# A channel DFT in even and odd halves, mirrored rows on GpSimd, padded tiles and a new order of the steps

## The chip, the cores and the metric

One core of one Trainium2 chip runs the whole program. The metric is the device time of one execution, in microseconds (us). Executions differ by more than a fraction of a per cent, so kernels are compared as ratios of fast executions from the same rounds on the same chip, with a 95% interval. Faster and slower mean by over 2%.

## The reference

Eight batches, each of 576 rows, with 8 heads of 64 dimensions: an attention with exponential features, then on its output `x` (576 x 512) a Fourier mixing, a normalisation and a feed-forward with 2048 hidden units.

```python
proj = einsum('bhsd,df->bhsf', x, w_phi); proj -= max(abs(proj), axis=-1)      # q and k
phi  = concatenate([exp(proj), exp(-proj)], axis=-1)
x    = (q_phi @ (k_phi^T v)) / (q_phi . sum(k_phi) + 1e-6)
u    = x + real(fft(fft(x, axis=seq), axis=channel))
un   = (u - mean(u)) / sqrt(var(u) + 1e-6)
out  = u + relu(un @ w_ch1) @ w_ch2
```

## The kernel before

In this program TensorE multiplies matrices and leaves the products in PSUM tiles; VectorE, ScalarE and GpSimd do the work element by element, and what isn't in PSUM lies in the working memory SBUF. A DFT is a discrete Fourier transform. The program is software-pipelined by hand. Each stream of work has a letter: F the feed-forward, M attention and mixing, D the folding of rows, N the normalisation, P, T, R and S the attention features, K, V and Q loads that GpSimd issues, A and B transposing DMAs, C constants, G and J the first transposes. Three strings of letters (a start, a first period, a period that is repeated) give the order in which the steps of different batches are issued. A step whose inputs or tile slots aren't ready by the plan is held and tried again at the next letter. Each engine then works through its own queue in that order, and what stands first in the queue holds up the rest (halfmm_k_ahead below shows it: GpSimd's queue stood 37.2 us in all at eight loads).

```python
def weave(plan):
    held = []
    for name in plan:
        held = [x for x in held if not step(x)]
        if name in held or not step(name):
            held.append(name)
...
BUFS = {"pj": 2, "pk": 1, "pb": 3}          # PSUM tiles; psf, pso and pu all come from pb
```

The part that is changed most is the channel DFT with the residual add. `DT` and `ET` hold the sequence transform, `CD` and `SD` are the cosine and sine matrices, `X` is the residual in SBUF (fp32), `C` = 512. Because of the symmetry of a real input one PSUM tile `pu` serves a direct row tile and its mirrored one, whose channels are read backwards.

```python
for t in range(3):
    M = 128 if t < 2 else 64
    pu = pb.tile([128, C], F32)
    ... 4 matmuls of 512 columns: DT.CD + ET.SD                       # L737
    if t < 2:
        nc.vector.tensor_tensor(out=X[:, t, 0:C], in0=pu[:], in1=X[:, t, 0:C], op=ALU.add)          # L742
        nc.vector.tensor_tensor(out=X[:, 2 + t, 1:C], in0=pu[:, C - 1:0:-1], in1=X[:, 2 + t, 1:C], op=ALU.add)   # L745
        nc.vector.tensor_tensor(out=X[:, 2 + t, 0:1], in0=pu[:, 0:1], in1=X[:, 2 + t, 0:1], op=ALU.add)
    else:
        nc.vector.tensor_tensor(out=X[0:64, 4, 0:C], in0=pu[0:64, :], in1=X[0:64, 4, 0:C], op=ALU.add)
```

After it come the statistics and the centred rows `UN` on VectorE, a transposing DMA to `UT`, the square roots `VE` and `rs` on GpSimd, and then the two matmul layers: `psf` (288 columns) from `UT`, and `pso` (512 columns), which VectorE adds to `X` (L832).

The softmax here doesn't subtract the row's maximum and nothing guards it: scores larger than these inputs give would overflow.

## Time and profile before

| | before |
|---|---|
| time | 461.1 us (456.46 to 462.73, 3 runs) |
| span of the profiled run, granted TensorE clock | 457.1 us, 0.946 |
| TensorE busy, idle (span less busy) | 409.4, 47.7 us |
| one steady period | 49.46 us, of which TensorE is busy 48.30, VectorE 38.83, ScalarE 36.11, GpSimd 33.63 |

The prediction below shows how these rows are read.

### The profile page before, as it was taken

To read this page: it belongs to the slowest core of one execution; us is meant where nothing else is said; L and a number is where in the kernel's file an instruction comes from. 1 tells how busy PE (TensorE), PEld (TensorE's weight loads), DVE (VectorE), ACT (ScalarE), POOL (GpSimd) and SP (SyncE) were. 2 spreads that over 40 slices of the span, in tenths; PEclk is the share of its full clock that TensorE was granted. 3 is DMA by queue.
4 is the path that set the end of the run, shared out by engine and by line. 5 is a ranking of instruction groups with operands and counts; after the bars stand their busy time and mean duration, and the time that the engine had idled before them with its cause. 6 is when DMAs were issued, how large, how long until landed. Compare 5 with 4: busy or idle time off the path is not lost.

```text
span 457.1 us, 10115 instructions
## 1 busy us (share of the span) xinstructions
PE 409.4 (90%) x3941; PEld 249.9 (55%) x3964; DVE 322.3 (71%) x597; ACT 303.2 (66%) x651; POOL 267.4 (58%) x357
## 2 busy tenths in 40 slices
PE   4586358889998999999999999999999999999994
PEld 3364125664367545764477436854576448645741
DVE  6868675695987678885887678877888585658012
ACT  5877468767865976587766885697658776621810
POOL 4867779369259683787367764778379433901000
PEclk9855576999999999999999999999999999999999
DMA  7699959905469086956599099908793052006004
GB/s 208 154 201 136 191 92 102 165 13 52 77 138 142 12 87 121 157 55 53 99 153 113 3 120 128 170 1 86 122 155 58 4 104 51 1 15 119 22 12 92
DMA packets 111087, 43.26 MB, mean 95 GB/s; under 512 B 85313, under 2 KB 105921, under 8 KB 111041
## 3 DMA queue, kind: packets, MB, share of 16 engines
q0 software_dynamic: 45936, 16.60, 34.4%
q1 hardware_dynamic: 65105, 26.03, 32.4%
q8 instruction: 31, 0.51, 0.5%
q14 instruction: 15, 0.12, 0.1%
HBM read 36.77 MB, written 9.44 MB: 101 GB/s over the span
## 4 chain that ended last, share of the span: by engine, by line
PE 65%; DMA 11%; DVE 9%; ACT 6%; POOL 5%; issue 2%; SPq 0%; DVEq 0%; ACTq 0%; POOLq 0%
PE pso L826 24%; PE psf L814 16%; PE pu L737 4%; DMA UT<-UN 3%; DMA QT<-QS 3%; PE psD L715 3%; PE kv L637 3%; PE pso L841 2%; PE psh L547 2%; POOL FEO L599 2%; DMA KT<-KS 2%; ACT HT L819 2%; PE psk L441 2%; PE psq L497 2%; ACT KPp L447 1%
## 5 line engine op out<-in xcount | busy, mean ns | idle before, releaser
L814 PE MATMUL psf<-UT,W1b 128*128 128x288 bf16 x1024 | 148.9, 288 | 6.9 <-DMA UT<-UN 4.6
L819 ACT ACTIVATE HT<-psf 128x288 bf16<-128x288 f32 x256 | 103.3, 413 | 57.9 <-PE psf L814 48.9
L826 PE MATMUL pso<-W2b,HT 128*128 128x512 bf16 x491 | 118.8, 380 | 1.4 <-issue 0.8
L814 PEld LDWEIGHTS <-W1b 128*128 128x128 bf16 x1024 | 92.5, 98 | 32.3 <-issue 10.0
L826 PEld LDWEIGHTS <-HT 128*128 128x128 bf16 x512 | 46.5, 98 | 56.5 <-issue 6.9
L667 POOL TENSOR_TENSOR X<-cb,rd 128x320 f32<-128x320 f32 x64 | 46.4, 729 | 35.8 <-DVE rd L666 35.8
L832 DVE SCALAR_TENSOR_TENSOR X<-pso,rs,X 128x512 f32<-128x512 f32 x32 | 24.0, 749 | 53.7 <-PE pso L826 53.6
L599 POOL TENSOR_TENSOR FEO<-X 128x320 f32<-128x320 f32 x59 | 49.6, 862 | 2.2
L416 POOL TENSOR_TENSOR VCn<-VS,VCn 128x512 bf16<-128x512 bf16 x28 | 29.8, 1066 | 34.3 <-ACT VCn L412 32.6
L505 DVE TENSOR_REDUCE MQ<-psq 128x8 f32<-128x1024 f32 (+1 forms) x40 | 39.4, 1005 | 10.3 <-PE psq L497 10.1
L461 DVE TENSOR_REDUCE MK<-psk 128x8 f32<-128x1024 f32 x32 | 38.5, 1218 | 6.7 <-ACT KPp L447 4.8
L788 POOL TENSOR_SCALAR VE<-MV 128x5 f32<-128x5 f32 x8 | 3.9, 488 | 65.4 <-DVE MV L766 65.3
L556 ACT ACTIVATE QPHP<-psh 128x1024 bf16<-128x1024 f32 x32 | 33.0, 1030 | 7.6 <-PE psh L547 7.5
L447 ACT ACTIVATE KPp<-psk 128x1024 bf16<-128x1024 f32 x32 | 32.6, 1019 | 1.4 <-PE psk L441 1.1
L447 ACT ACTIVATE KPn<-psk 128x1024 bf16<-128x1024 f32 x32 | 32.6, 1018 | 1.0 <-DVE MK L461 1.0
L556 ACT ACTIVATE QPHN<-psh 128x1024 bf16<-128x1024 f32 x32 | 33.1, 1036 | 0.0
L416 POOL TENSOR_TENSOR VCp<-VS,VCp 128x512 bf16<-128x512 bf16 x28 | 31.2, 1114 | 0.0
L645 ACT CAST kvh<-kv 128x130 bf16<-128x130 f32 x64 | 17.4, 272 | 20.3 <-PE kv L641 20.3
L652 PEld LDWEIGHTS <-QPHP 128*128 128x128 bf16 x320 | 24.8, 102 | 5.5 <-DVE cb L664 4.3
L765 DVE BATCH_NORM_STATS2 st<-X 128x6 f32<-128x512 f32 (+1 forms) x40 | 27.4, 685 | 0.3
L652 PEld LDWEIGHTS <-QPHN 128*128 128x128 bf16 x320 | 23.2, 99 | 1.3 <-issue 0.2
L237 POOL DMA_DIRECT2D QS<-in_q_dram x28 | 23.1, 837 | 0.3 <-issue 0.3
(404 smaller groups left out, 746.9 us busy)
## 6 DMA issues: line engine op xcount, KB each, us to landing
out_dram<-X SPq DMA_DIRECT2D x64, 64.0 KB
out_dram<-X SPq DMA_DIRECT2D x16, 256.0 KB
KS<-in_k_dram POOLq DMA_DIRECT2D x14, 256.0 KB, 7.3
QS<-in_q_dram POOLq DMA_DIRECT2D x14, 256.0 KB, 5.0
VS<-in_v_dram POOLq DMA_DIRECT2D x7, 512.0 KB, 9.7
W1b<-in_moe_w_ch_dram POOLq DMA_DIRECT2D x1, 2048.0 KB, 12.9
W2b<-in_moe_w_ch_dram POOLq DMA_DIRECT2D x1, 2048.0 KB, 21.4
W2b<-in_k_dram SPq DMA_DIRECT2D x2, 512.0 KB
```

The lines of the kernel that those rows point to most:

```text
L416: nc.gpsimd.tensor_tensor(out=VC[:, hs, :, 0:D], in0=values[b][0][:, hs, :].rearrange("p h (j d) -> p h j d", d=D), in1=VC[:, hs, :, D:D + ...
L447: nc.scalar.activation(out=KP[:, hs, :, :].rearrange("p e (jp jj) f -> p jj (e jp) f", jj=2), in_=psk[:], func=AT.Exp, scale=sgn,)
L461: nc.vector.tensor_reduce(out=MK[:, 2 * pr:2 * pr + 2, :].rearrange("p e (jp jj) -> p jj (e jp)", jj=2), in_=tiles[pr][:], axis=AX.X, op=A ...
L505: nc.vector.tensor_reduce(out=o, in_=i[:], axis=AX.X, op=ALU.max, apply_absolute_value=True)
L556: nc.scalar.activation(out=o, in_=psh[:], func=AT.Exp, scale=sgn)
L599: eng.tensor_tensor(out=FEO[:, :, i, a:a + D], in0=X[:, :, a:a + D], in1=X[:, :, C - a:C - a - D:-1], op=op,)
L652: nc.tensor.matmul(pn_[:, i, 65 * c:65 * c + 65], lhsT=QP[:, h, 128 * c:128 * c + 128], rhs=kvh[:, i, :], start=True, stop=True,)
L667: nc.gpsimd.tensor_tensor(out=X[:, :, D * h:D * h + D], in0=cb[:, :, 0:D], in1=rd[:].to_broadcast([128, 5, D]), op=ALU.mult,)
L765: nc.vector.bn_stats(out=st[0:M, :], in_=X[0:M, c, 0:C])
L814: nc.tensor.matmul(ps[:], lhsT=W1b[:, cc, 128 * hh:128 * hh + 128], rhs=UT[:, cc, 288 * hf:288 * hf + 288], start=(cc == 0), stop=(cc == N ...
L819: nc.scalar.activation(out=HT[:, hh, 288 * hf:288 * hf + 288], in_=ps[:], func=AT.Relu)
L826: nc.tensor.matmul(po[:], lhsT=HT[:, hh, 128 * c:128 * c + 128], rhs=W2b[:, hh, :], start=(hh == 0), stop=(hh == NHH - 1),)
```

## The change

Its intent: fewer columns on TensorE in the channel DFT. The cosine part is even in the channel and the sine part odd, so 257 and 255 columns suffice, and sum and difference of the two give both halves of a row. The diff, cut to its core:

```diff
-START = "CGGTCRTGGRJJGSSTTTWC ... "      # all plans are new; the last three batches get their own
+START = "PGGTDSTCSTCCGTGQRJGT ... "
+LAST = "KRMFFTMFMFMFMPFMPFMF ... "
-        weave(START + FIRST + PERIOD * (B - 1))
+        weave(START + FIRST + PERIOD * (B - 3) + LAST)
...
+            if b:
+                half_channels(X, FEO, t)
+                yield
+                continue
...
+    def half_channels(X, FEO, t):
+        pu = pb.tile([128, C], F32, tag="pb", name="pu")
+        n = C // 2
+        ... 3 matmuls of 257 columns into pu[:, 0:n+1], 2 of 255 into pu[:, n+1:C]
+        nc.scalar.copy(out=QO[0:M], in_=pu[0:M, n + 1:C])                              # L798, to SBUF
+        for i, op in enumerate((ALU.add, ALU.subtract)):
+            nc.vector.tensor_tensor(out=PQ[0:M, i, 1:n], in0=pu[0:M, 1:n], in1=QO[0:M], op=op)   # L801
+        nc.scalar.copy(out=PQ[0:M, 0, 0:n + 1:n], in_=pu[0:M, 0:n + 1:n])              # L804
+        adds = [(nc.vector, X[0:M, c, 0:n + 1], PQ[0:M, 0, :]),
+                (nc.vector, X[0:M, c, n + 1:C], PQ[0:M, 1, n - 1:0:-1])]
+        if t < 2:
+            adds += [(nc.gpsimd, X[:, 2 + t, 1:n], PQ[:, 1, 1:n]),
+                     (nc.gpsimd, X[:, 2 + t, n:C], PQ[:, 0, n:0:-1]),
+                     (nc.gpsimd, X[:, 2 + t, 0:1], PQ[:, 0, 0:1])]
+        for eng, x, y in adds:
+            eng.tensor_tensor(out=x, in0=x, in1=y, op=ALU.add)                         # L817
```

`QO` and `PQ` lie in SBUF, in the room of `FEO`. Besides: the one-row and one-column matmuls `pm` and `px` and the 64-row `pu` become full tiles, the big K load is issued ahead of the small one at the start, four 960-element constants move from VectorE to GpSimd, and eight small exponentials a batch become four. Batch 0 keeps the full channel DFT.

## The prediction

> **What bounds the kernel now.** I read the page's busy shares first, then the slices, the chain that ended last, the stretches of one steady period, and last the matmul timeline of that period.
>
> ```profile
> span 457.1 us, 10115 instructions
> PE 409.4 (90%) x3941; PEld 249.9 (55%) x3964; DVE 322.3 (71%) x597; ACT 303.2 (66%) x651; POOL 267.4 (58%) x357
> PE   4586358889998999999999999999999999999994
> PEclk9855576999999999999999999999999999999999
> PE 65%; DMA 11%; DVE 9%; ACT 6%; POOL 5%; issue 2%; SPq 0%; DVEq 0%; ACTq 0%; POOLq 0%
> ```
>
> Two regimes. In the first seven slices of 11.4 us (to about 80 us) TensorE is loosely filled and has a granted clock near 0.5; from there to 451 us it is the bound, nine tenths or more busy at full clock. The chain agrees: 65% of it is TensorE. One steady period (one batch), cut where the same stage recurs, is the first line below; columns are the stretch, its length, then busy us of PE, PEld, DVE, ACT, POOL, the clock, DMA share and GB/s.
>
> ```profile
> 247.92:297.38 49.46, 48.30 (x489) 29.16 (x491) 38.83 (x70) 36.11 (x80) 33.63 (x42) 1.00 0.76 99
> ```
>
> TensorE idles 1.2 us of 49.5; VectorE has 10.6 us to spare, ScalarE 13, GpSimd 16. So a period gets shorter only by giving TensorE less to do. "Busy" hides a part, because matmul records overlap; the starts show it:
>
> ```profile
> 254.22 1.47 PE L826 MATMUL pso<-W2b,HT 128*128 128x512 bf16 x6
> 255.62 0.38 PE L692 MATMUL pm<-HI,ones_b 1*128 1x512 bf16 x1
> 255.94 1.04 PE L826 MATMUL pso<-W2b,HT 128*128 128x512 bf16 x4
> 256.91 0.40 PE L441 MATMUL psk<-wphi,KT 64*128 64x128 bf16 x8
> 257.24 4.06 PE L826 MATMUL pso<-W2b,HT 128*128 128x512 bf16 x18
> ...
> 268.45 0.60 PE L737 MATMUL pu<-CD,DT 128*128 128x512 bf16 x2
> 268.89 0.59 PE L737 MATMUL pu<-SD,ET 128*128 128x512 bf16 x2
> 269.32 1.46 PE L826 MATMUL pso<-W2b,HT 128*128 128x512 bf16 x6
> ```
>
> From 257.24 the 18 second-layer matmuls run to 261.14, where the next group starts: 0.216 us each. Six from 254.22 should end at 255.52; the one-row pm starts at 255.62, and the full-tile stream resumes at 255.94, not 255.83. So each change of tile shape (128*128 to 1*128, to 64*128, and back) costs about 0.104 us, unseen in the busy column. Four pu matmuls take 268.45 to 269.32, 0.87 us, with no such gap.
>
> At the start I look at where the chain leaves TensorE:
>
> ```profile
> 46.78 2.20 POOL VS L237 x3
> 49.92 1.44 POOL CD L213 x2
> 51.36 1.14 POOL SD L213 x2
> 53.70 0.67 POOL SE L613
> 54.39 0.70 DVE CEO L697
> ```
>
> Batch 0's folding (SE) sits on GpSimd behind DMA issues and the making of constants.
>
> **What the Trainium skill says.** "TensorEngine Tiling (Array Packing)", section Key Properties: "Changing tiling mode (not just tile) drains the TensorE". The trace agrees, with the 0.104 us above. "TensorE: Matmul & The Clock Gate", section Back-to-back issue gap: N/2.4 + 2.5 ns when warm, 216 ns for N = 512; the trace has 0.216. I use it for N = 257 and 255, which no row shows. "VectorE: DVE Perf Modes", section on the trn2 errata: a fp32 tensor_tensor takes (N+151)/0.96 ns; 691 ns for 512, and the 128x512 add from PSUM has 688 here. "GPSIMD Engine Reference", section Engine selection: GpSimd has no PSUM port; that explains why the mirrored adds need a copy in SBUF first. No row of the kernel before tests that.
>
> **The change part by part.**
>
> Half channels (batches 1 to 7). Removed per batch: 12 matmuls of 512 columns, 12 x 0.216 = 2.59 us. Added: per row tile three of 257 (0.1096 us) and two of 255 (0.1088 us), 0.546 us; three tiles 1.64 us. TensorE saves 0.95 us a batch, 6.7 us in seven.
>
> Its price elsewhere, per batch. VectorE: before 2 x (0.688 + 0.680 + 0.148) + 0.682 = 3.71 us; after, four operations of about 256 elements per tile, each (256+151)/0.96 = 0.424 us, so 12 x 0.424 = 5.09: plus 1.4. ScalarE: three copies of 255 columns (128x130 takes 0.272 and 128x288 0.413 here, so about 0.38 in between) and three of two elements (0.2, as the smallest activations here): plus 1.75; against that 8 exponentials of 128x8 become 4, minus 4 x 0.23 = 0.9. GpSimd: per tile of the first two, two adds of 256 (SE, 128x256, took 0.67) and one of a column (0.19): 2 x 1.53 = plus 3.1. None is near its limit: VectorE goes to 40.2 us, ScalarE 37.0, GpSimd 36.7, in a period of at least 47. It lies beside TensorE, except that the X rows come later: pu now goes matmul, ScalarE copy, VectorE, then GpSimd, perhaps 2 us more before the statistics of the mirrored rows.
>
> Padded tiles. pm (1 row), px (1 column) and the last pu (64 columns) become full tiles at the same columns. That removes four shape changes a batch in the plan, 0.4 us.
>
> The new order. I mapped each letter of the plans to the tile shape of its matmuls and counted changes of shape in the order written. The old PERIOD has 33 per batch with padding not counted; the new PERIOD 19 (padding included): its T and P steps, the 64-row ones, stand together. So 14 fewer per period, 14 x 0.104 = 1.46 us, with the 0.95: 2.4 us in each of five periods, 12.0 us. FIRST goes from 47 to 31: 1.7 + 0.95 = 2.6 us. In the last two forwards nearly no T and P is left (8 against 3 changes): 0.5 + 0.95 = 1.5 us. Sum on TensorE 16.1 us. Letters that aren't ready are held and run later, so the count is a plan and not an order; some of it will be missed.
>
> Start. The first K load was the fourth to be issued, at 2.85 us, and landed 4.0 us later; now it is issued first, near 0.8, so its transposes could start near 5 instead of 6.9 us: about 1.5 us. Four 960-element constants leave VectorE (3.6 us) for GpSimd, which stood idle for 7.9 us until 13.3. The CD/SD step (C) now stands after the second fold (D) in the plan, so 3.9 us of GpSimd work move behind SE; W2b's issue (1.2) comes in front, SDX (about 1.3) behind. I book 1.5 us there, in all 3 us.
>
> Gross: 16.1 + 3 = 19 us. I take some four fifths, 15.5 us: the held letters, a fuller VectorE (86% of a 47 us period) and the longer pu path will take some back.
>
> **Rivals.**
> (a) VectorE or the pu path takes TensorE's place: with 6.8 us to spare per period instead of 10.6, bursts (sums, norms, maxima of K) could make TensorE wait for PSUM buffers. For: in 255 to 279 us VectorE already runs with few gaps and the tile pool has three buffers. Against: only some 0.9 us a period of TensorE's idle time is a wait for anything now. It would keep a third of the gain: about 455 us.
> (b) Only the arithmetic and the padding count, the order is neutral: 6.7 + 2.6 + 1.5 at the start: about 450 us.
> (c) Everything counts and the order also removes the present 1.2 us of idle time per period and waits of batches 0 to 1 (10 us of idle time between 80 and 440 in the 20 us stretches): about 438 us.
> (d) The start gets worse: the W1b issue moves from the 19th to the 69th letter, so its 12.9 us landing may collide with batch 1's loads and delay the first feed-forward (69 us): some us lost, about 450.
>
> **Range and chances.** 461.1 - 15.5 = 445.6. Range 438 (c) to 453 (between b and a). Two per cent lies at 451.9; the runs before scatter from 456.5 to 462.7, so the limit itself may be 450. I give 0.82 to faster, 0.17 to within 2%, 0.01 to slower.
>
> **What would show it.** The steady period falls from 49.46 to about 47.2 us with TensorE still idle under 1.5 us and at clock 1.00; pu groups become five starts in about 0.55 us; pm and px stand in the full-tile stream without a gap; 64*128 groups follow each other. VectorE busy per period about 40, GpSimd about 36.7. In the chain before 60 us the CD/SD rows are gone. Wrong, if the period stays above 48.3 with new TensorE waits on pu's readers, or on UT behind GpSimd's adds (a), if shape changes cost the same number of gaps as before (b), or if the first psf comes later than 69 us because of W1b (d).

## More of the kernel before

Behind the bar stand the busy us of the whole group and the mean ns of one instruction, then the idle time of the engine ahead of it.

```profile
L742 DVE TENSOR_TENSOR X<-pu,X 128x512 f32<-128x512 f32 x16 | 11.0, 688 | 1.2 <-PE pu L737 0.5
L613 DVE TENSOR_TENSOR SE<-FEO 128x384 f32<-128x384 f32 x7 | 8.0, 1144 | 0.0
L613 DVE TENSOR_TENSOR SE<-FEO 128x128 f32<-128x128 f32 x7 | 2.0, 280 | 0.0
```

A fp32 add of 512 columns from PSUM takes 0.69 us. The fold `SE` reads both of its inputs from SBUF, and its two shapes don't fit together: 128 columns take 0.28 us, so 384 should take less than the 512 of L742, and they take 1.14.

## The result and the profile after

| | before | after |
|---|---|---|
| time, median | 461.64 us (4 runs) | 481.41 us (479.49 to 484.71, 4 runs) |
| ratio | 1 | 1.0454, interval 1.037 to 1.0539: slower |
| span of the profiled run, clock | 457.1, 0.946 | 478.9, 0.945 |
| TensorE busy, idle | 409.4, 47.7 | 402.5, 76.4 |

A ratio is the mean time of one kernel's fast runs over that of the kernel before's fast runs in the same rounds, so it isn't quite the ratio of the medians. Executions over 1.5% slower than the fastest of the same kernel are left out of the means.

The last row of the table is the whole result. TensorE's work fell by 6.9 us, and its idle time rose by 28.7: together the 21.8 us by which the span grew. The page of the changed kernel (busy shares, and shares of the chain):

```profile
PE 402.5 (84%) x3962; PEld 256.6 (54%) x3985; DVE 345.3 (72%) x628; ACT 305.7 (64%) x661; POOL 303.0 (63%) x413
...
PE 40%; DVE 28%; DMA 15%; ACT 9%; issue 3%; POOL 2%; SPq 1%; DVEq 0%; ACTq 0%; POOLq 0%
```

In the chain that ended last (second row) TensorE's share fell from 65 to 40%, and VectorE's rose from 9 to 28%. Three periods, cut at the same stage as before (the 64-row `pso`):

```profile
183.66:238.58 54.92, 48.16 (x491) 30.17 (x493) 46.02 (x79) 36.51 (x82) 36.85 (x48) 0.97 0.65 91
238.58:287.41 48.83, 46.48 (x491) 29.86 (x494) 39.90 (x71) 36.23 (x81) 37.16 (x48) 1.00 0.73 94
287.41:343.34 55.93, 49.01 (x491) 30.37 (x494) 46.73 (x80) 37.01 (x84) 36.84 (x48) 0.94 0.63 89
```

They last 53.2 us in the mean, not 47.2. GpSimd (36.9) and ScalarE (36.6) are where the prediction had them, VectorE isn't: 44.2 in the mean, not 40.2. Its groups by shape say which operations:

```profile
L817 DVE TENSOR_TENSOR X<-X,FEO 128x255 f32<-128x255 f32 x14 | 17.3, 1233 | 0.0
L817 DVE TENSOR_TENSOR X<-X,FEO 128x257 f32<-128x257 f32 x14 | 14.8, 1054 | 3.2 <-ACT FEO L804 3.2
L801 DVE TENSOR_TENSOR FEO<-pu,FEO 128x255 f32<-128x255 f32 x28 | 10.5, 417 | 4.7 <-ACT FEO L798 4.6
L817 DVE TENSOR_TENSOR X<-X,FEO 64x257 f32<-64x257 f32 x7 | 2.9, 420 | 1.5 <-ACT FEO L804 1.5
```

All four have the same length. L801 (one input in PSUM) and the 64-row L817 take 0.42 us, as predicted. The 128-row L817, with both inputs in SBUF, takes 1.05 and 1.23. What is different about it stands in the timelines of VectorE and GpSimd over the same 15 us:

```profile
225.56 5.11 DVE L817 TENSOR_TENSOR X<-X,FEO 128x257 f32<-128x257 f32 x2 [0.23 <-ACT FEO L804]
...
233.40 0.74 DVE L894 SCALAR_TENSOR_TENSOR X<-pso,rs,X 128x512 f32<-128x512 f32 x1
...
235.04 1.73 DVE L817 TENSOR_TENSOR X<-X,FEO 128x257 f32<-128x257 f32 x2 [0.23 <-ACT FEO L804]
...
239.11 0.75 DVE L817 TENSOR_TENSOR X<-X,FEO 64x257 f32<-64x257 f32 x2 [0.22 <-ACT FEO L804]
```

```profile
225.61 1.06 POOL L438 TENSOR_TENSOR VCp<-VS,VCp 128x512 bf16<-128x512 bf16 x1
226.62 1.74 POOL L817 TENSOR_TENSOR X<-X,FEO 128x255 f32<-128x255 f32 x3
228.33 1.05 POOL L438 TENSOR_TENSOR VCn<-VS,VCn 128x512 bf16<-128x512 bf16 x1
229.35 1.05 POOL L438 TENSOR_TENSOR VCp<-VS,VCp 128x512 bf16<-128x512 bf16 x1
234.89 1.93 POOL L817 TENSOR_TENSOR X<-X,FEO 128x255 f32<-128x255 f32 x3 [4.49 <-DVE FEO L801]
```

A pair of direct adds takes 0.75 us where GpSimd rests (the 64-row one at 239.11) and 1.73 beside GpSimd's own mirrored adds (235.04). It takes 5.11 beside a run of GpSimd that goes on without a gap to 230.40: scalings of V (VCn, VCp), the mirrored adds, and two scalings more. VectorE gets its second add done 0.27 us after that run has ended. In the third period a pair takes 5.12 us again. In the middle one, the period of 48.83 us, the pair at 278.88 takes 1.74: the same parts stand on GpSimd there too, but the pair starts 0.46 us into a scaling that the mirrored adds follow, and the slow pair 0.97 us into one that another scaling follows. Of the 14 pairs of 128 rows in the trace, 12 take 1.63 to 1.75 us and two take 5.1. Against the 0.75 us of a free pair, the 12 ordinary ones lose some 12 us together and the two long ones 9.

The chain shows what the late adds hold up (start, us, what):

```profile
225.56 5.13 DVE X L817 x2
...
233.49 0.66 DVE X L894
...
244.31 0.52 POOL VE L850
...
246.10 5.69 DMA KS<-in_k_dram
...
251.80 2.57 DMA KT<-KS
```

From 224.6 to 244.2 this chain is VectorE's, save three ScalarE copies of 0.2 us. Two things hang on it. The evacuation of `pso` (L894) at 233.49 stands behind the adds in VectorE's queue, and it gives back the PSUM tile that the next `pu` needs. And the last statistics release GpSimd's `VE` and `rs`, which stand ahead of the issue of the next K load in GpSimd's queue. TensorE's waits (us in all, times, longest) name the first, and the transposes behind `UN` and the K load:

```profile
PE pu L790 <- DVE X L894: 11.4, 6, 3.7
PE psf L876 <- DMA UT<-UN: 8.1, 4, 3.9
PE pst L345 <- DMA HT<-in_k_dram: 6.8, 1, 6.8
PE ps L449 <- DMA KT<-KS: 6.8, 5, 2.1
```

To see where the difference arises I note for each kernel when each batch's 64-row `pso` starts. Before: first at 125.6 us, then intervals of 50.2, 49.3, 49.7, 49.5, 49.4, 42.5, 33.0. After: first at 130.2, then 53.5, 54.9, 48.8, 55.9, 51.4, 41.9, 35.1. So 4.6 us are lost in the start and most of the rest in the full periods. "Period" below means these intervals. They are read from one trace of each kernel; those of full_k_ahead, full_k_mid and no_mirrored_adds were taken in slow runs.

### The profile page after: what moved, and what is told of

The parts are those of the page before. It is cut to its first block, busy times and chain, and to the rows that moved or that the text cites. A ratio compares the mean times of both kernels' runs of the same rounds, so it can differ in the third digit from the quotient of the medians.

```text
span 478.9 us, 10268 instructions
## 1 busy us (share of the span) xinstructions
PE 402.5 (84%) x3962; PEld 256.6 (54%) x3985; DVE 345.3 (72%) x628; ACT 305.7 (64%) x661; POOL 303.0 (63%) x413
## 4 chain that ended last, share of the span: by engine, by line
PE 40%; DVE 28%; DMA 15%; ACT 9%; issue 3%; POOL 2%; SPq 1%; DVEq 0%; ACTq 0%; POOLq 0%
PE psf L876 14%; PE pso L888 13%; DVE X L817 6%; DMA KS<-in_k_dram 6%; DVE st L827 4%; DMA KT<-KS 4%; DVE UN L836 3%; DVE FEO L801 2%; PE psk L463 2%; DMA UT<-UN 2%; DMA QT<-QS 2%; ACT KPp L469 2%; DVE MK L483 2%; DVE X L910 2%; PE psD L735 2%
## 5 line engine op out<-in xcount | busy, mean ns | idle before, releaser
L881 ACT ACTIVATE HT<-psf 128x288 bf16<-128x288 f32 x256 | 102.1, 415 | 48.6 <-PE psf L876 40.4
L888 PE MATMUL pso<-W2b,HT 128*128 128x512 bf16 x490 | 124.0, 387 | 1.5 <-issue 0.9
L876 PEld LDWEIGHTS <-W1b 128*128 128x128 bf16 x1024 | 94.0, 99 | 37.5 <-issue 14.4
L888 PEld LDWEIGHTS <-HT 128*128 128x128 bf16 x512 | 48.1, 100 | 54.1 <-issue 8.4
L689 POOL TENSOR_TENSOR X<-cb,rd 128x320 f32<-128x320 f32 x64 | 46.6, 733 | 40.7 <-DVE rd L688 40.2
L621 POOL TENSOR_TENSOR FEO<-X 128x320 f32<-128x320 f32 x59 | 50.8, 880 | 2.2
L817 POOL TENSOR_TENSOR X<-X,FEO 128x255 f32<-128x255 f32 (+2 forms) x42 | 26.1, 649 | 32.6 <-DVE FEO L801 32.6
L483 DVE TENSOR_REDUCE MK<-psk 128x8 f32<-128x1024 f32 x32 | 38.9, 1219 | 10.6 <-ACT KPn L469 6.7
L894 DVE SCALAR_TENSOR_TENSOR X<-pso,rs,X 128x512 f32<-128x512 f32 x32 | 23.7, 745 | 28.3 <-PE pso L888 28.3
L817 DVE TENSOR_TENSOR X<-X,FEO 128x257 f32<-128x257 f32 (+3 forms) x42 | 36.2, 901 | 4.7 <-ACT FEO L804 4.7
L850 POOL TENSOR_SCALAR VE<-MV 128x5 f32<-128x5 f32 x8 | 3.9, 487 | 49.5 <-DVE MV L828 49.4
L804 ACT COPY FEO<-pu 128x2 f32<-128x2 f32 (+1 forms) x21 | 3.4, 160 | 42.6 <-DVE FEO L801 42.6
## 6 DMA issues: line engine op xcount, KB each, us to landing
W1b<-in_moe_w_ch_dram POOLq DMA_DIRECT2D x1, 2048.0 KB, 17.3
```

Source lines behind the costliest of these rows:

```text
L483: nc.vector.tensor_reduce(out=MK[:, 2 * pr:2 * pr + 2, :].rearrange("p e (jp jj) -> p jj (e jp)", jj=2), in_=tiles[pr][:], axis=AX.X, op=A ...
L621: eng.tensor_tensor(out=FEO[:, :, i, a:a + D], in0=X[:, :, a:a + D], in1=X[:, :, C - a:C - a - D:-1], op=op,)
L689: nc.gpsimd.tensor_tensor(out=X[:, :, D * h:D * h + D], in0=cb[:, :, 0:D], in1=rd[:].to_broadcast([128, 5, D]), op=ALU.mult,)
L817: eng.tensor_tensor(out=x, in0=x, in1=y, op=ALU.add)
L876: nc.tensor.matmul(ps[:], lhsT=W1b[:, cc, 128 * hh:128 * hh + 128], rhs=UT[:, cc, 288 * hf:288 * hf + 288], start=(cc == 0), stop=(cc == N ...
L881: nc.scalar.activation(out=HT[:, hh, 288 * hf:288 * hf + 288], in_=ps[:], func=AT.Relu)
```

## The experiments

Eighteen kernels ran. The ratio is always that to the kernel before; kernels marked "wrong" give a wrong result.

| kernel | median us | ratio | interval |
|---|---|---|---|
| full_dft | 455.5 | 0.9916 | 0.9852 to 0.998 |
| half_old_order | 507.6 | 1.1014 | 1.097 to 1.1058 |
| adds_on_pool | 479.8 | 1.0414 | 1.0341 to 1.0486 |
| adds_from_psum | 467.3 | 1.0129 | 1.0076 to 1.0182 |
| half_matmuls_only (wrong) | 455.9 | 0.9719 | 0.9628 to 0.9811 |
| full_old_order | 471.8 | 1.0186 | 1.0105 to 1.0266 |
| full_old_start | 467.4 | 1.0102 | 1.0039 to 1.0164 |
| sbuf_adds | 488.2 | 1.0567 | 1.0482 to 1.0652 |
| psum_copy | 482.3 | 1.0457 | 1.0348 to 1.0567 |
| full_k_ahead | 476.5 | 1.0325 | 1.0243 to 1.0408 |
| halfmm_k_ahead (wrong) | 475.1 | 1.0268 | 1.0171 to 1.0365 |
| half_k_ahead | 499.6 | 1.0706 | 1.0611 to 1.0802 |
| pq_hop_only (wrong) | 452.7 | 0.9775 | 0.9716 to 0.9834 |
| pq_no_hop (wrong) | 462.4 | 1.0019 | 0.9967 to 1.007 |
| full_k_mid | 454.5 | 0.9827 | 0.9779 to 0.9876 |
| full_unpadded | 456.8 | 0.9876 | 0.9827 to 0.9926 |
| no_mirrored_adds (wrong) | 469.8 | none | |
| halfmm_k_mid (wrong) | 448.7 | 0.9752 | 0.9689 to 0.9815 |

The medians take in slow runs, the ratios don't: of half_matmuls_only's four runs two were fast, 447.85 and 451.38 us, and two slow.

### Which part: the half channels, or the order?

full_dft is the changed kernel with the full channel DFT for all batches.

```diff
-            if b:
+            if False:
                 half_channels(X, FEO, t)
```

> The changed kernel with its own order, start and padding, but every batch with the full-width channel DFT of the kernel before (no half channels). Theory P (shared port: VectorE's adds of two SBUF tensors stall while GpSimd works, pu and pso wait behind them): the steady period falls from 50 to 57 us to about 48.5 or less, total about 460 us, since the loss of the start stays. Theory O (the new order and start are the cause): stays above 473 us, with the same waits for K and Q loads.

Measured: 0.9916. The half channels therefore cost 5.4 points (1.0454 less 0.9916), some 25 us, and everything else together gains under 1%. In the two traces 8.5 us of the distance lie ahead of the end of the first batch (130.2 us against 121.7) and 15.4 in the five periods. A steady period of full_dft:

```profile
223.93:272.08 48.15, 47.12 (x489) 29.60 (x491) 38.37 (x70) 35.71 (x76) 33.45 (x42) 1.00 0.78 105
```

half_old_order is the changed kernel with the plans of before; it shows whether the new order is to blame.

```diff
-        weave(START + FIRST + PERIOD * (B - 3) + LAST)      # new plans
+        weave(START + FIRST + PERIOD * (B - 1))             # the three plans of before
```

> The changed kernel with the three plans of the kernel before (no own last periods). Theory P: the half-channel adds collide with GpSimd's scaling of V in the old order too, so it stays slow, 468 us or more, with adds of over 0.8 us on average. Theory O: near the kernel before, 455 to 462 us.

Measured: 1.1014, 47 us over the kernel before. The new order isn't to blame. Periods are 55 to 57 us without it. Against full_old_order (1.0186, below) the half channels cost 8.3 points in the old order and 5.4 in the new; the rest of the 47 us is the new code without its own start.

### What in the half channels: the matmuls, or the price?

half_matmuls_only keeps the five half-width matmuls and takes the adds of before, so that TensorE has its saving and no other engine pays. The result is wrong, the timing is meant.

```diff
-        nc.scalar.copy(out=QO[0:M], in_=pu[0:M, n + 1:C])
-        ... PQ and the adds of the change
+        if t < 2:
+            nc.vector.tensor_tensor(out=X[:, t, 0:C], in0=pu[:], in1=X[:, t, 0:C], op=ALU.add)
+            ... the adds of before
```

> The changed kernel with the five half-width matmuls per tile, but the adds of the kernel before straight from the PSUM tile (the result is wrong on purpose). If the term of the prediction for TensorE (0.95 us a batch) was right and the loss is all in what follows the matmuls: 6 to 7 us below full_dft (455.5), so about 449 us. If the smaller matmuls bring nothing: 455 us.

Measured: 0.9719, span 445.9. The cheaper matmuls are worth 5.7 us of span against full_dft (451.6 less 445.9), and the ratios put it at 2.0 points, with intervals of nearly a point each way; 6.7 us were counted. But they are not worth it in the steady period:

```profile
171.85:219.96 48.11, 46.49 (x492) 29.87 (x495) 39.82 (x69) 35.69 (x76) 33.27 (x42) 1.00 0.78 100
```

TensorE is busy 0.63 us less than in full_dft and the period is as long. The gain lies in the first batch, the first period and the fifth (120.1, 51.7 and 48.5 us, against 121.7, 54.1 and 50.7).

The distance from here to the changed kernel is the price: 1.0454 less 0.9719, 7.35 points, some 34 us. The next kernels divide it.

### The price: the shared port

"Port" stands here for whatever VectorE's second SBUF input shares with GpSimd; the page that names it is cited further below, under why the prediction was wrong. adds_from_psum writes sum and difference back into the PSUM tile and does all five adds on VectorE from PSUM. GpSimd has no part in it, no VectorE add of this step has two inputs in SBUF, and the second ScalarE copy (L804) falls away (not in the cut).

```diff
+        nc.vector.tensor_tensor(out=pu[0:M, n + 1:C], in0=pu[0:M, 1:n], in1=QO[0:M], op=ALU.subtract)
+        nc.vector.tensor_tensor(out=pu[0:M, 1:n], in0=pu[0:M, 1:n], in1=QO[0:M], op=ALU.add)
...
-            eng.tensor_tensor(out=x, in0=x, in1=y, op=ALU.add)          # x, y in SBUF
+            nc.vector.tensor_tensor(out=x, in0=y, in1=x, op=ALU.add)    # y in pu
```

> The changed kernel, but sum and difference are written back into the PSUM tile and all five adds are done by VectorE from there, one SBUF input each: seven VectorE operations on a tile in place of four, none on GpSimd. Theory P: each add takes 0.41 to 0.45 us whatever GpSimd does, no 5 us stalls, total about 463 us though VectorE has more operations. Theory W (VectorE simply has too many operations in this step): worse than the changed kernel, 485 us or more.

Measured: 1.0129, correct. VectorE now does more operations and needs less time; the group of the direct 128x257 adds:

```profile
L813 DVE TENSOR_TENSOR X<-pu,X 128x257 f32<-128x257 f32 x14 | 6.0, 427 | 0.5
```

The same 128x257 add takes 0.427 us from PSUM, and took 1.054. So 3.25 points (1.0454 less 1.0129), 15 us, are the price of sending the second input of the adds through SBUF and half of the adds to GpSimd. The second copy's share in it was not run alone; VectorE waited 4.7 us in all for it in the changed kernel (the rows with L804).

adds_on_pool gives GpSimd the direct adds too, so that VectorE needs no port for them.

```diff
-            (nc.vector, X[0:M, c, 0:n + 1], PQ[0:M, 0, :]),
-            (nc.vector, X[0:M, c, n + 1:C], PQ[0:M, 1, n - 1:0:-1]),
+            (nc.gpsimd, X[0:M, c, 0:n + 1], PQ[0:M, 0, :]),
+            (nc.gpsimd, X[0:M, c, n + 1:C], PQ[0:M, 1, n - 1:0:-1]),
```

> The changed kernel, but the two direct-row adds per tile go to GpSimd as well; VectorE has none of the five. Theory P: no VectorE add of two SBUF tensors is left in this step, so its 5.1 us stalls go; GpSimd is later by some 4 us a batch: total about 465 us. A theory that only counts VectorE work (36 us for these adds in all) expects the same direction, so this run alone does not tell them apart. Theory O: within 1% of the changed kernel (481).

Measured: 1.0414, no different from the changed kernel. VectorE is freed of the adds, but the rows now come from GpSimd's queue, behind the scaling of V, and VectorE's statistics wait for them at the head of its own queue (28.6 us in all). TensorE's wait for `pu` behind L894 is 12.6 us in all, where it was 11.4. Taking the port away from one side only moves the lateness.

no_mirrored_adds leaves out GpSimd's two wide adds per tile.

```diff
-                (nc.gpsimd, X[:, 2 + t, 1:n], PQ[:, 1, 1:n]),
-                (nc.gpsimd, X[:, 2 + t, n:C], PQ[:, 0, n:0:-1]),
```

> The changed kernel without GpSimd's two wide mirrored adds per tile (wrong result on purpose; its one-column add stays). If VectorE's adds standing still beside the scaling of V is the cost: the adds of 255 stay near 1 us on average with single ones of some 4 us, total 472 us or more. If the lateness and the traffic of GpSimd's own adds is: the total falls to about 465 us, that of adds_from_psum.

Inconclusive on the total: three of its four runs count as slow (465.5, 474.1 and 483.4 us, against 457.1), and no ratio was given. Its rows do say something:

```profile
L815 DVE TENSOR_TENSOR X<-X,FEO 128x257 f32<-128x257 f32 x14 | 13.6, 970 | 3.2 <-ACT FEO L804 3.2
L815 DVE TENSOR_TENSOR X<-X,FEO 128x255 f32<-128x255 f32 x14 | 5.8, 416 | 0.0
```

The second add is back at 0.416 us, the first isn't. Nine of the 14 pairs take 0.76 us, beside at most GpSimd's one-column add, although both inputs lie in SBUF as before. Three that start during a scaling of V take 1.2, and two take 3.9: the one at 238.21 stands between scalings that run from 233.16 to 241.46 with only a one-column add among them. The two rows sum to 19.4 us here, to 32.1 in the changed kernel and to some 12 if no add is slowed. So most of the slowing, 13 of 20 us, came with the mirrored adds that the change itself brought, and the scaling of V, which was there before, slows the first add of five pairs. These are durations of single instructions in the trace of a slow run; what they were worth in the total isn't shown.

sbuf_adds tries the port in the kernel before, without any half channels: ScalarE copies `pu` to SBUF and the old adds read the copy.

```diff
+            PC = FEO[:].rearrange("p c i n -> p (c i n)")[:, C * t:C * (t + 1)]
+            nc.scalar.copy(out=PC[0:M], in_=pu[0:M])
-                    out=X[:, t, 0:C], in0=pu[:], in1=X[:, t, 0:C], op=ALU.add
+                    out=X[:, t, 0:C], in0=PC[:], in1=X[:, t, 0:C], op=ALU.add
```

> The kernel before with one change: ScalarE copies pu to SBUF first and VectorE's adds of the same widths read two SBUF tensors. Theory P (a VectorE add of two SBUF tensors waits while GpSimd works): the adds, 0.69 us now, go above 1.0 us on average with single ones of 2 us and more, and the whole is slower by 10 us or more. Theory W (only the number of operations counts): the adds stay near 0.69 us; only the copy (0.6 us on ScalarE, which has 13 us to spare a period) is added: within 3 us of the kernel before.

psum_copy is its control: the same copy, in place in PSUM, so that the adds wait for ScalarE in the same way and read PSUM as before.

```diff
+            nc.scalar.copy(out=pu[0:M], in_=pu[0:M])
```

> Control for sbuf_adds: the kernel before with the same copy by ScalarE ahead of the adds, but back into the PSUM tile, so the adds wait for it just the same and have one SBUF input. Theory P: adds back at 0.68 us, total 461 to 469 us against 488 of sbuf_adds. If the wait for the copy made sbuf_adds slow: 480 us or more.

Measured: 1.0567 and 1.0457. The rows of sbuf_adds, then of psum_copy:

```profile
L747 DVE TENSOR_TENSOR X<-FEO,X 128x511 f32<-128x511 f32 x16 | 16.9, 1058 | 0.0
L744 DVE TENSOR_TENSOR X<-FEO,X 128x512 f32<-128x512 f32 x16 | 14.1, 880 | 15.7 <-ACT FEO L742 15.7
```

```profile
L743 DVE TENSOR_TENSOR X<-pu,X 128x512 f32<-128x512 f32 x16 | 11.1, 692 | 16.0 <-ACT pu L741 16.0
L746 DVE TENSOR_TENSOR X<-pu,X 128x511 f32<-128x511 f32 x16 | 10.9, 680 | 0.0
```

The mean of the single add rises with two SBUF inputs (0.88 and 1.06 us, against 0.69 and 0.68), in a kernel where GpSimd does nothing new: the port is confirmed as a cause of slow adds. One by one in the trace, each of these adds that has no GpSimd instruction beside it takes 0.68 to 0.69 us, as before, and those slowed, 1.1 to 1.5, all stand beside a scaling of V. But my expectation for the control was far off. Nearly all of the loss of sbuf_adds is in psum_copy too. VectorE stands 16 us in all before L743, with the head of its queue waiting for a copy of ScalarE. In the plan of before this hop (512 columns in eight batches) costs 4.6%, 21 us, and the port only 1.1 points more, with intervals that overlap.

### The price: the hop over ScalarE, and the number of operations

These two again, in the new order. pq_hop_only is half_matmuls_only with an in-place ScalarE copy of the odd half (255 columns, seven batches) ahead of the adds; pq_no_hop is adds_from_psum without that copy, reading stale data.

```diff
+        nc.scalar.copy(out=pu[0:M, n + 1:C], in_=pu[0:M, n + 1:C])     # pq_hop_only, over half_matmuls_only
...
-        nc.scalar.copy(out=QO[0:M], in_=pu[0:M, n + 1:C])              # pq_no_hop, over adds_from_psum
```

> half_matmuls_only (wrong result on purpose, 451 us in its fast runs) with one thing more: ScalarE copies the 255 odd columns of pu in place in PSUM before VectorE's adds, as the changed kernel must copy them to SBUF. VectorE has no operation more. If the wait for ScalarE's queue is the cost: most of the 20 us up to adds_from_psum, 463 us or more. If the number of VectorE operations is: 451 to 455 us.

> adds_from_psum without ScalarE's copy (VectorE adds whatever lies in that scratch, so the result is wrong on purpose): all seven VectorE operations, no wait for ScalarE. If the hop is the cost: 453 to 457 us. If VectorE's operations are: 463 us or more, near adds_from_psum.

Measured: 0.9775 and 1.0019. Adding the hop costs 0.6 points (0.9775 less 0.9719), taking it away gains 1.1 (1.0129 less 1.0019): 3 to 5 us, and the smaller figure is within the intervals. The traces have it ahead of the end of the first batch, which comes at 126.6 us with the hop and at 120.1 in half_matmuls_only. In all fast traces with the new START this end lies at 119.8 to 121.7 us in the six kernels without the hop and at 123.3 to 130.2 in the five with it. In the periods no price of the hop shows: the first five sum to 246.0 us in pq_hop_only and 245.3 in half_matmuls_only, to 253.8 in adds_from_psum and, without the hop, to 260.8 in pq_no_hop. Why the start pays it stays open. (The traces of pq_hop_only and pq_no_hop are those of their slowest fast runs, so the size is better taken from the ratios.) The rest of the distance, with or without the hop, goes with VectorE's longer list of operations: 1.0019 less 0.9719 is 3.0 points, 1.0129 less 0.9775 is 3.5, so 14 to 16 us. In adds_from_psum the pu step has 18 operations a batch, worth 47.9 us in seven batches or 6.8 each (the rows of L799, L800 and L813 summed), against 7 operations and 3.7 us before. Three microseconds more a batch on an engine that is busy 41 of 50 us thus cost about two. Whether it is their number or their time isn't separated.

### Where the rest of the expected gain went: start, order, padding

full_old_order is full_dft with all plans of before; full_old_start has the old START and FIRST, and the new PERIOD and LAST.

```diff
-            if b:
+            if False:
-START = "PGGTDSTCSTCC ... "; FIRST = "NMPTVRTTPMFF ... "     # both kernels
+START = "CGGTCRTGGRJJ ... "; FIRST = "PMFTKMPTRFTM ... "
-PERIOD = "BMFFMFMFMFSM ... "; weave(... PERIOD * (B - 3) + LAST)   # full_old_order only
+PERIOD = "MKFMFFMFPMFP ... "; weave(... PERIOD * (B - 1))
```

> The changed kernel with full-width DFT and the three plans of the kernel before: only the edits of the start, the padding, the merged exponentials and the move of constants remain. If the new order gives what was counted (about 1.46 us a period), this is 5 to 10 us slower than full_dft, 461 to 465 us; the padding alone would make it 2 to 3 us faster than the kernel before, 458 us.

> Full-width DFT with the START and FIRST of the kernel before, then the new PERIOD and LAST. Tells whether the new start helps: full_dft ends its first forward 3.8 us earlier than the kernel before and loses 4 us in the next interval. If the start plan is worth it: 457 to 461 us; if not: 452 us or less.

Measured: 1.0186 and 1.0102. With the old start the first `psf` comes at 82 us (69.0 before, 73.1 in full_dft): the new code without its own order makes the start 13 us worse. It seems that the changed constants, loads and conditions were fitted to the new START; which of them it is wasn't run. The periods of full_old_order are 49.3 to 50.9, as before, and those of full_old_start 48.0 to 49.5 up to the fourth. So the new PERIOD is what shortens the steady period: 48.1 us in full_dft against 49.26, 49.73 and 49.46 before, 1.4 us in the mean. 1.46 were counted from changes of tile shape. The traces have these changes: with TensorE's matmuls in order of start, and up to 32 rows or columns taken as 32 and up to 64 as 64, a period has 32 changes before, 18 in full_dft and in the changed kernel, and 29 in full_old_order. So all 14 came about, and held letters took nothing back.

full_unpadded is full_dft with `pm`, `px` and the last `pu` in small tiles again.

```diff
-        nc.tensor.matmul(pm[:], lhsT=ones_b[:], rhs=HI[:], start=True, stop=True)
+        nc.tensor.matmul(pm[:], lhsT=ones_b[0:1], rhs=HI[0:1], start=True, stop=True)
...
-                px[:], lhsT=CX[:, c, :] if c < 2 else CEO[0:65, 2, 1, 0:128],
+                px[0:1, :], lhsT=CX[:, c, 0:1] if c < 2 else CEO[0:65, 2, 1, 0:1],
```

> full_dft with pm, px and the last pu in their small tiles again (one row, one column, 64 columns). By the count of shape changes in the prediction (0.104 us each, four a batch): 3 us slower than full_dft, 458.5 us. If the period hangs on a loop that TensorE does not set: no difference.

Measured: 0.9876, against 0.9916 with padding: not told apart. Its steady periods are 48.35 to 48.53, some 0.35 us longer than full_dft's, about the 0.4 that four changes were counted at; over three steady periods that is 1 us of 455. By the count above it has 24 changes a period, six more than full_dft, which makes 0.06 us each; full_old_order has 11 more and periods 1.9 us longer, 0.17 each. The price of 0.104 us fits the sum of the 14 and not these two parts, so that the changes of shape are the whole of the 1.4 us isn't shown.

### What holds the new steady period

half_matmuls_only left a riddle: less work and the same period. Its chain has the K load in three of its periods (at 227, 276 and 324 us), and the plan issues it from GpSimd, behind `rs`. The next kernels issue it earlier. The first three put a K into FIRST, which moves every later K load ahead by a period: in full_dft, in half_matmuls_only (wrong) and in the changed kernel.

```diff
-FIRST = " ... FFMFFPPBFMFFFFFNFFFT ... "
+FIRST = " ... FFMFFPPBKFMFFFFFNFFFT ... "
```

> full_dft with one letter more: a K put into FIRST behind its B, so that the K rows of every later batch are loaded a whole period before their transposes instead of just ahead of them. Theory L (in the new order the steady period is a loop: end of a forward, statistics, GpSimd's rs, issue of the K load behind it, K load, K transposes, keys of the next batch, its mixing): the 48.1 us periods become about 47.3 us and the 54.1 us one shorter, total about 449 us. If TensorE's own work sets the period: within 1 us of full_dft (455.5).

> half_matmuls_only (wrong result on purpose) with the same K ahead. Its periods are 48.1 us like those of full_dft although TensorE has 0.95 us less to do. Theory L: with the loop broken they fall to about 46.5 us, a microsecond below those of full_k_ahead; total about 443 us. If another thing holds the period at 48.1: total about 450 us.

> The changed kernel as it is, with the same K ahead. Theory L: part of its loss is that the longer way from pu to the statistics lies on the loop through the K load; with K ahead it gains more than full_k_ahead does, 8 us or more: about 470 us; the stalls of the adds beside GpSimd (5 us ones) remain. If only the stalls matter: 478 us or more.

Measured: 1.0325, 1.0268 and 1.0706, all far slower where I had expected a gain. A line of TensorE's waits in halfmm_k_ahead, one of several alike, once a period, and one of GpSimd's:

```profile
PE pn__3035 L674 <- DVE cb L686: 6.3, 1, 6.3
POOL KS L255 <- DMA KT<-KS: 37.2, 8, 9.3
```

The load now stands in GpSimd's queue before its target buffer is free (the transposing DMA that reads the old K rows hasn't ended), and everything behind it in that queue stands too. The experiment tested a wrong place, not the idea. full_k_mid and halfmm_k_mid (wrong) mend it: the K in FIRST, and PERIOD's K moved from its 14th place to just ahead of V.

```diff
-PERIOD = "BMFFMFMFMFSMPKPMFMFSMSMFMFFMFFMFMFFPTPPFFFMFFVMM ... "
+PERIOD = "BMFFMFMFMFSMPPMFMFSMSMFMFFMFFMFMFFPTPPFFFMFFKVMM ... "
```

> full_dft with the K rows loaded a period ahead (a K more in FIRST) as in full_k_ahead, but the K of PERIOD moved from its 14th place to just ahead of V, where the K transposes of the batch have long been done, so its issue does not hold GpSimd's queue. Theory L (the period hangs on the K load): periods of 47.3 us in place of 48.1 and of 50.7 before the last two, total about 449 us. If TensorE or another loop sets the period: 455 us as full_dft.

> half_matmuls_only (wrong result on purpose) with the plan of full_k_mid. If the K load holds the steady period at 48.1 us: about 47.2 us a period, and a total some 1.5% below full_k_mid, 0.968 of the kernel before. If another loop holds it: periods of 48 us and 0.975 or more.

Measured: 0.9827 and 0.9752. The early K doesn't shorten the period: halfmm_k_mid has 48.51, 48.65 and 48.50, with no K load in its chain, and full_k_mid 48.6 to 48.9. So the K load isn't what holds half_matmuls_only's period at 48.1, and what does stays open. full_k_mid has the lowest ratio of the correct kernels, 1.7% below the kernel before and 6% below the changed one. Its interval lies under 1, and on both sides of the 2% line; from full_unpadded and full_dft it is not told apart.

## Why the prediction was wrong

It gave 0.82 to faster and 445.6 us; it was 481.4.

**The step that failed** is "None is near its limit: VectorE goes to 40.2 us, ScalarE 37.0, GpSimd 36.7, in a period of at least 47. It lies beside TensorE", and in it first of all the term "12 x 0.424 = 5.09". Half of it was right: sum and difference took 0.417 us. The 28 direct adds of 128 rows took 1.05 and 1.23. VectorE's part of the pu step came to 7.7 us a batch (53.6 us, the rows of L801 and L817 summed, over seven). The duration was carried over from adds with one input in PSUM to adds with both in SBUF, beside a busy GpSimd. The runs show this twice: adds_from_psum brings the same add from 1.054 back to 0.427 us and takes back 3.25 points (with the mirrored adds off GpSimd and the second copy gone), and sbuf_adds slows the old adds in the kernel before. The Trainium skill says it plainly, in "SBUF — State Buffer", section Who interferes with whom: a DVE instruction with two SBUF inputs contends with a GpSimd instruction that reads SBUF, and the loser is fully blocked for the whole instruction. The prediction cited the GpSimd page for the missing PSUM port and drew from it only that a copy is needed. The trace of before had the sign: the `SE` row at 1144 ns for 384 columns, each of the seven beside a GpSimd instruction.

**"It lies beside" failed even without the port.** adds_from_psum has no port conflict in these adds and is still 1.3% slower than the kernel before and 4.1 points slower than half_matmuls_only: 3.0 to 3.5 of them with VectorE's longer list of operations, 0.6 to 1.1 for the hop over ScalarE. VectorE had 10.6 us to spare in a period, but not between `pu` and the statistics. There its queue has no gaps, and `pso` tiles, the transposes and, through `rs`, the next K load wait for its end. Spare time in another part of the period is of no use to that. The "perhaps 2 us more" for late rows was this term: in the trace above the chain is 19.6 us on VectorE, and TensorE stood 3.7 us before one `pu`.

**Rival (a)** had the direction, VectorE and the pu path in TensorE's place, and the signs it gave are those that came: a period above 48.3, waits on pu's readers. Its size (a third of the gain kept, 455 us) was far off, because it too took the 0.42 us for granted.

**What was right.** TensorE's saving: 6.7 us counted for the half channels, 5.7 found in the spans of half_matmuls_only and full_dft, and the whole of TensorE's busy time fell by 6.9. The 0.55 us of the five matmuls: in the trace they start at 227.51 and the next group at 228.07. The new order: 14 changes of shape fewer a period and 1.46 us counted, 14 fewer and 1.4 us found in full_dft, padding included; that the price of one is 0.104 us throughout isn't borne out. In half_matmuls_only the two don't add up: the prediction has 47.2 us a period for both together, and it stayed at 48.1.

**The start** didn't gain its 3 us. The prediction looked at the big K block, whose transposes started at 6.90 us; those of the small one stand ahead of them in TensorE's queue and had started at 3.69. The small block is now the later load, so its transposes start at 6.85 us and the big block's at 7.44. The first `psf` came at 74.8 us, not 69.0, and in full_dft at 73.1, so rival (d) has 4 to 6 us there, though full_dft makes up for it before the end of the first batch (121.7 against 125.6) and loses that again in the first period (54.1 against 50.2). But its reason fails: W1b, issued at 39.6 us, had landed by 56.9 (17.3 us, 12.9 before), and the first `psf` waits for the transposing DMA to `UT`. W2b was landing beside that DMA, from 50.6 to 73.9 us; that it delayed it is only argued. Two readings of the prediction were loose as well: the clock of the first seven slices reads 9855576, so it is near 0.5 in three of them alone, and the 0.67 us taken for a 128x256 `SE` is its piece of the chain, of an instruction of 0.71.

**Open.** What exactly decides whether a pair of direct adds takes 1.7 or 5.1 us (the slow ones meet one scaling of V behind another); why the start pays for the hop; what holds half_matmuls_only's steady period at 48.1 us; and whether the K load behind `rs`, which the chain of the changed kernel shows in each full period, would free it if issued at the better place: only the bad place was run there. The terms of the price (15 us, 14 to 16, 3 to 5) are differences along one row of kernels, so that they add up to the 34 proves nothing, and the first holds several parts. The plan matters to them too: the hop was 21 us in the plan of before, with the wider copy, and 3 to 5 in the new one.

## What to carry to other kernels

Take an operation's duration from a row with the same operand places and the same neighbours on the other engines, and not with the same length alone: a VectorE add with both inputs in SBUF isn't the one that reads PSUM. Before work is moved "beside" the bound, look at the stretch in which it must be done, because an in-order queue has no spare time where its results are awaited. And run the saving without its price first: half_matmuls_only shows that the most to be had from the half matmuls was about 2%, while the new order with the full DFT and the K load moved lay 1.7% below the kernel before, without that price.

## What the Trainium skill lacked or had wrong

- "SBUF — State Buffer" states the lock between VectorE and GpSimd for two SBUF inputs, and the runs agree with it. It has the loser wait until the first has finished, and doesn't say what becomes of it when the next instruction follows at once. Here an add of 0.42 us became 1.05 and 1.23 in the mean, and the one at 225.56 was done at 227.72, after three GpSimd instructions had ended during it (at 225.66, 226.67 and 227.35), so that one lost lock can be followed by another.
- "VectorE: DVE Perf Modes", section on the trn2 errata: its (N+151)/0.96 ns held for adds with an input in PSUM (0.415 to 0.427 us for 255 to 257 columns) and for 64 rows beside an idle GpSimd. It failed by a factor of two to three for two SBUF inputs beside a busy one, and the section has no word of that condition next to the formula.
- "TensorEngine Tiling (Array Packing)", section Key Properties: the drain at a change of tiling mode has no size there. Here it was 0.104 us in the kernel before, and a plan with 14 changes fewer a period was 1.4 us a period shorter; 6 and 11 changes in other kernels went with 0.35 and 1.9 us.
- No page that I read gives the price of one more engine in a chain of in-order queues. Here a ScalarE copy ahead of VectorE's three steps a batch cost 21 us in one order of the steps (512 columns) and 3 to 5 in another (255 columns).
